# One block of weight sums moved a step forward, and one row load moved from the x products to the y products

## The chip, the cores and the metric

The kernel runs on one core of a Trainium2 chip. The metric is the device time of one execution in microseconds. The kernel before takes 1419.04 us (median of three runs, 1418.62 to 1419.61). The engines that matter here are TensorE (PE, the matrix products), VectorE (DVE), ScalarE (ACT) and SyncE (SP), which issues all transfers. Each engine works through its own list of instructions in order; an instruction that waits holds up all that stand behind it in that list.

## The reference

Two layers are applied one after the other to x, of 2048 rows by 512 columns, each with two sublayers:

```
x = x + A(layernorm(x))     A: y = Cr @ (x @ Dr^T) - Ci @ (x @ Di^T)
x = x + B(layernorm(x))     B: h = gelu(layernorm(x) @ w1); shift four column groups of h
                               by +1, -1, +2, -2 rows; x1 = x + shifted @ w2
                               return x1 + gelu(layernorm(x1) @ w3) @ w4
```

Cr and Ci are the 2048 x 2048 cosine and sine matrices, Dr and Di the 512 x 512 ones; w3 is 512 x 1376 and w4 is 1376 x 512. All is float32.

## The kernel before

**Products in three parts.** Every float32 operand is split into a high part (a cast on ACT) and a low part (a subtraction on DVE), and every product is three matmuls: high by high, high by low, low by high (`mm3`, lines 295 to 297). So PE's work is fixed, and ACT and DVE have to split every operand in time.

**Sublayer A.** The output rows are worked in four chunks of 512 columns (c = 0 to 3). A chunk has first the x products, in steps 0 to 15 (`x_phase`: an even step is two groups of six matmuls into the PSUM banks psc and psb, an odd step one group into psa), and then the y products, k = 0 to 7 (`y_phase`: per k two steps of twelve matmuls, into psc and psd and then psb and psa). Between the x steps of chunks 1 to 3 stand the hidden products of the chunk before, into psd. At the end of the x products ACT copies psc, psb and psa out to SBUF (rr11f L518, rr01f L520, rr00f L526); the first y product writes psc again and so waits for the first of these copies.

**The stream.** The DFT matrices come from HBM in pieces of 512 KB into four buffers (raw0 to raw3), six during the end of the x products and the y products. `stage_one` makes from a piece, or a difference of two (L247, on DVE), what goes into one of four ring slots and casts its high part (L241, L244, L248, on ACT); `stage_two` subtracts to get the low part (L258, on DVE). `stream()` runs this as far ahead as there is a free ring slot. A raw buffer's next load is issued on SP once DVE and ACT have read it.

**Order.** The schedule is written by hand: the order of the calls is the order on each engine. Before each step a `hook` is called, which adds other work at that place. In layer 0 the hook of the x products calls `prepare_at(c, i)`: beside the products of chunks 1 to 3, sums and differences of blocks of w3 and w4 are formed for later. A unit has four parts: `sum_load` (two loads of 256 KB, L1629), `sum_make` (one addition of 512 and two of 256 elements per partition on DVE, L492, and a cast of 1024 on ACT, L1646), `sum_low` (a subtraction of 1024 on DVE, L1650) and `sum_keep` (the store). Chunks 1 and 2 have three units each; the third uses the tile tmp (`sum_t`), which is loaded at x step 11, once tmp's former contents have been stored.

**Rows that come back.** In each layer's last chunk pairs of rows of x are read back from HBM into xs tiles: `BACK` gives the x step and the row. xs[2] (rows 4 and 5) is next read by `norm_z((4, 5))` among the hidden products behind the y products.

Of the kernel before, what the change touches and what calls it, by code (L numbers as in the profile page):

```python
# [21 lines left out]
NC = S // CH  # L22
# [14 lines left out]
WARM = 12  # L37
X6, X7 = 2, 4
HAT = (2, 3, 3, 4, 5, 5, 6, 6)
BACK = {8: 0, 11: 2, 13: 4}  # L40
HORDER = ((1, 0), (0, 1), (1, 1), (0, 0))


# [1 line left out]
def spectral_mlp_kernel(ctx: ExitStack, tc: tile.TileContext, x, ws, hs, w1, w2, w34, out):  # L45
# [10 lines left out]
    x1d = dram.tile([S, D], F32, name="x1d")  # L56
# [28 lines left out]
    def at(name, word, *shape, dtype=F32R):  # L85
        return nc.alloc_sbuf_tensor_at(name, [P, *shape], dtype, offset=base + 4 * word).ap()
# [11 lines left out]
    xs = [at(f"xs{i}", XS + i * 2 * D, 2, D, dtype=F32) for i in range(NP)]  # L98
# [26 lines left out]
    def xt(j):  # L125
        return xs[j // 2][:, j % 2]
# [77 lines left out]
    def rows(sb, d, j, n, load):  # L204
        v = d[j * P : (j + n) * P, :].rearrange("(t p) d -> p t d", p=P)
        nc.sync.dma_start(*((sb, v) if load else (v, sb)))
# [146 lines left out]
    def normed_act(o, s, mr):  # L353
        nc.scalar.activation(o, s, AF.Identity, bias=mr[2], scale=mr[1])
# [100 lines left out]
    late = {}  # L455

    def plain_phase(hook):

        for k in range(NP):
            first, last = k == 0, k == NP - 1  # L460
            a = {"11": ay[k][:, 2], "22": ay[k][:, 3], "21": mid[k % 4][:, 0], "12": mid[k % 4][:, 1]}
            s = stream()
            hook(2 * k)
            jobs = ((PB, a["21"], s[:, 1]), (PA, a["11"], s[:, 1]), (PC, a["12"], s[:, 0]), (PD, a["22"], s[:, 0]))
            if first:
                mm_first(jobs[:2])
                mm_first(jobs[2:])
            else:
                for job in jobs:
                    mm_half(*job, False, False)  # L470
            s = stream()
            hook(2 * k + 1)
            mm_half(PC, a["11"], s[:, 1], False, last)
            mm_half(PD, a["21"], s[:, 1], False, last)
            mm_half(PB, a["22"], s[:, 0], False, last)
            mm_half(PA, a["12"], s[:, 0], False, last)
# [153 lines left out]
    def turn_one(t, q, u):  # L630
        v = t.rearrange("p d (a q j) -> p d a q j", a=NB, q=TC)[:, :, :, q]
        nc.vector.transpose(v, blocks_of(u))

    def turn_out(t, to=None):

        if to is None:
            count["turn"] += 1
            to = zd[count["turn"] % 2]
        z = to.rearrange("(e i) t -> i e t", i=B)
        for b in range(NB):  # L640
            v = t[b * B : (b + 1) * B].rearrange("i d (a t) -> i (d a) t", a=NB)
            nc.sync.dma_start(z[:, :, b * P : (b + 1) * P], v)

    def turn_in(dst):

        z = zd[count["turn"] % 2].rearrange("(d p) t -> p d t", p=P)
        nc.sync.dma_start(dst[:, :, 1], z)
# [971 lines left out]
    sum_t = tmp[:, 0:4].rearrange("p u (a w) -> p u a w", a=2)  # L1619
    sum_t = [(sum_t.bitcast(F32R), sum_t, slice(0, 4))]  # L1620

    def sum_load(kind, k, places):


        src = w34[2 * k : 2 * k + 2, :, 0] if kind == 3 else w34[2 * k + LAG : 2 * k + LAG + 2, :, 1]
        for _, f, v in places:
            for i in range(2):
                if v.start <= 2 * i < v.stop:
                    nc.sync.dma_start(f[:, 2 * i - v.start : 2 * i - v.start + 2, 0], src[i].rearrange("p (a w) -> p a w", a=2))  # L1629

    def sum_make(kind, places):


        raw = [f[:, j, 0] for _, f, v in places for j in range(v.stop - v.start)]
        form = [f[:, j, 1] for _, f, v in places for j in range(v.stop - v.start)]
        r11, r12, r21, r22 = raw if kind == 3 else [raw[i] for i in (0, 2, 1, 3)]
        if len(places) == 1:
            f = places[0][1]
            add(f[:, 0:4:3, 1], r21.unsqueeze(1).broadcast_to([P, 2, 2 * P]), f[:, 0:4:3, 0])
        else:  # L1640
            add(form[0], r21, r11)
            add(form[3], r21, r22)
        add(form[1], form[3], r11)
        add(form[2], form[1], r12)
        for t, f, _ in places:
            nc.scalar.copy(t[:, :, 0], f[:, :, 1])  # L1646

    def sum_low(places):
        for t, f, _ in places:
            nc.vector.tensor_tensor(t[:, :, 1], f[:, :, 1], t[:, :, 0].bitcast(F32), op=ALU.subtract)  # L1650

    def sum_keep(kind, k, places):
        for t, _, v in places:
            if kind == 4:
                nc.sync.dma_start(w4s[k][:, v], t.bitcast(F32))
                continue
            for r in range(2):
                nc.sync.dma_start(w3d[k][:, r, v], t[:, :, r].bitcast(F32))
# [3 lines left out]
    def sum_at(c, kind, k, places, *at_):  # L1662
        todo = (
            lambda: sum_load(kind, k, places),
            lambda: sum_make(kind, places),
            lambda: sum_low(places),
            lambda: sum_keep(kind, k, places),
        )
        for step, f in zip(at_, todo):
            prepare.setdefault((c, step), []).append(f)  # L1670

    def prepare_at(*at_):
        for f in prepare.pop(at_, ()):
            f()

    for c, units in ((1, ((3, 0), (3, 1), (3, 2))), (2, ((3, 3), (3, 4), (4, 0))), (3, ((4, 1), (4, 2)))):
        sum_at(c, *units[0], sum_b, 5 if c == 1 else 0, 8 if c == 1 else 7, 9 if c == 1 else 8, 9)
        sum_at(c, *units[1], sum_a, 1, 10, 11, 12 if c == 3 else 21)
        if c < 3:
            sum_at(c, *units[2], sum_t, 11, 13, 14, 18)  # L1680
    sum_at("hid", 4, 3, sum_b, 0)
    sum_at("hid", 4, 4, sum_r, 2)

    for layer in range(LAYERS):
# [4 lines left out]
        for c in range(NC):  # L1689
            if layer == 0 and c == 0:  # L1690
# [58 lines left out]
                def hook(i):  # L1749
                    k, odd = divmod(i, 2)  # L1750
                    prepare_at(c, i)
                    if not i:
                        second_low(1)
                        xp_stats(1)
                        second_low(0)
                        state["two"] += 1
                        issue_dma()
                        state["limit"] = 4
                        prefetch()
                    state["limit"] = w_items[layer]  # L1760
                    if not odd:
                        if k + 1 < NP:
                            xp_norm(k + 1, 3)
                            xp_main(k + 1)
                        if not k:
                            xp_main_lows(1)
                    else:
                        if 0 < k < NP - 1:
                            xp_main_lows(k + 1)
                        if k + 2 < NP:  # L1770
                            xp_stats(k + 2)
                        if k:
                            xp_sums(k - 1)
                            xp_highs(k - 1, False)
                            xp_lows(k - 1, False)
                    w_split(i)
# [3 lines left out]
            def hook(i):  # L1780
# [34 lines left out]
                if i == 9:  # L1815
                    rows(X0, x1d, j, 2, False)
                if c == NC - 1 and i in BACK:
                    rows(xs[BACK[i] // 2], x1d, BACK[i], 2, True)
                if c == NC - 1 and i == 12:
# [5 lines left out]
            def hook(k):  # L1825
                if layer == 0:
                    prepare_at(c, 2 * NP + k)
                if layer and c == 0:
                    for step, f in zip((1, 1, 2), (ay_sums, ay_highs, ay_lows)):
                        if k == step:  # L1830
                            f(7)
                if k == 1 and c:
                    rows(X1, x1d, (c - 1) * TC + 2, 2, False)
                if c == NC - 1 and k < 2:
                    for q in (2 * k, 2 * k + 1):
                        turn_one(turned0, q, tmp[:, q])
                    for j in (2, 3)[: 2 - 2 * k]:
                        normed_act(tmp[:, j], xt(j), ln2[j])
                if c == NC - 1 and k == 2:
                    turn_out(turned0)  # L1840
                if c == NC - 1 and k == NP - 1:
                    turn_in(ztf[0])

# [86 lines left out]
```

## Time and profile before

| | |
|---|---|
| median of three runs | 1419.04 us |
| the profiled execution's own time | 1418.97 us |
| its span, first to last instruction | 1417.2 us |
| PE busy | 1409.0 us, 99% of the span |
| PE's granted clock | full in all 40 slices |
| DVE busy | 1191.3 us, 84% |
| ACT busy | 765.5 us, 54% |
| transfers | 316.18 MB, mean 223 GB/s |

The span lies 1.8 us under the execution's own time; nothing in the change touches what lies around it. PE is busy nearly throughout, so the time of a stage is PE's work plus the few places where PE stands still. In a timeline a row is: start in us, length in us, engine, line, operation, output and inputs with their shapes, how many instructions are merged, and in brackets the idle time before it with what ended it. Instructions of one engine overlap by a little: the distance of two starts is what an instruction costs its queue. Chunk 1 of layer 0 has its change from x to y products at about 149 us, chunk 2 at 248 us, chunk 3 at 347 us.

### The profile page before, as it was taken

Reading aid. Unit: us, or ns where it says so; the run is one execution under the profiler, and the core shown is the slowest. Engines: PE = TensorE matmul, PEld = TensorE weight load, DVE = VectorE, ACT = ScalarE, POOL = GpSimd, SP = SyncE. Lnnn points to the kernel's source line nnn. Section 1 sums busy time; section 2 is a strip of 40 time slices with the busy share of each in tenths; the row PEclk is TensorE's granted clock in tenths of the full one; section 3 lists DMA queues with packets and bytes.
Section 4 is the critical chain, followed back from the end, with each engine's and each line's share of the span. In section 5 each row is a group of like instructions: output and inputs, shape, how many; then the busy total and the mean of one; then the engine's idle time right before and its main releaser. Section 6 shows DMA issues by size and latency. Waiting matters only on the chain.

```text
span 1417.2 us, 18479 instructions
## 1 busy us (share of the span) xinstructions
PE 1409.0 (99%) x6669; PEld 1181.8 (83%) x6669; DVE 1191.3 (84%) x1684; ACT 765.5 (54%) x1072; POOL 68.2 (5%) x105
## 2 busy tenths in 40 slices
PE   9999999999999999999999999999999999999998
PEld 8888788888788888988888888888888888899887
DVE  7988998998988789956789979879889788897776
ACT  6664555556566655534555545645555566454351
POOL 2100000000001100000000000000000020000000
PEclk9999999999999999999999999999999999999999
DMA  8978858778774748865556476565587457687864
GB/s 290 306 236 302 268 194 274 241 230 309 255 228 146 253 165 264 257 247 180 195 177 218 136 225 206 166 220 170 193 265 237 134 141 245 188 250 252 297 205 160
DMA packets 158907, 316.18 MB, mean 223 GB/s; under 512 B 10848, under 2 KB 78816, under 8 KB 156896
## 3 DMA queue, kind: packets, MB, share of 16 engines
q1 hardware_dynamic: 158816, 315.01, 67.9%
q8 instruction: 52, 0.85, 0.2%
q14 instruction: 39, 0.32, 0.1%
HBM read 260.70 MB, written 54.26 MB: 222 GB/s over the span
## 4 chain that ended last, share of the span: by engine, by line
PE 94%; DVE 3%; DMA 1%; ACT 1%; issue 1%; SPq 0%; POOL 0%; DVEq 0%; ACTq 0%; POOLq 0%
PE psd L295 10%; PE psd L296 10%; PE psd L297 10%; PE psa L295 8%; PE psa L297 8%; PE psa L296 8%; PE psb L296 7%; PE psb L297 7%; PE psb L295 7%; PE psc L295 6%; PE psc L296 6%; PE psc L297 6%; DMA raw<-in_ws 1%; DVE ring L258 1%; DVE rest L492 0%
## 5 line engine op out<-in xcount | busy, mean ns | idle before, releaser
L241 ACT CAST ring<-raw 128x1024 fp32r<-128x1024 f32 x127 | 132.9, 1052 | 69.4 <-PE psd L297 30.6
L258 DVE TENSOR_TENSOR ring<-raw,ring 128x1024 fp32r<-128x1024 f32 x126 | 153.4, 1220 | 14.3 <-ACT ring L241 14.3
L295 PE MATMUL psd<-ring,rr 128*128 128x512 f32 x208 | 80.9, 389 | 0.0
L296 PE MATMUL psd<-ring,rr 128*128 128x512 f32 x208 | 80.9, 389 | 0.0
L297 PE MATMUL psd<-ring,rr 128*128 128x512 f32 x208 | 80.9, 389 | 0.0
L248 ACT CAST ring<-ring0f 128x1024 fp32r<-128x1024 f32 x28 | 29.5, 1054 | 46.9 <-DVE ring0f L247 46.9
L258 DVE TENSOR_TENSOR ring<-ring1f,ring 128x512 fp32r<-128x512 f32 (+1 forms) x56 | 53.3, 952 | 0.8 <-ACT ring L244 0.7
L346 POOL TENSOR_TENSOR rows<-ve,mhalf 128x4 f32<-128x4 f32 x16 | 18.2, 1136 | 735.2 <-DVE ve L345 735.2
L295 PE MATMUL psc<-ring,ay 128*128 128x512 f32 x128 | 50.0, 391 | 1.6 <-ACT rr11f L518 1.6
L296 PE MATMUL psb<-ring,ay 128*128 128x512 f32 x128 | 50.0, 391 | 1.2 <-DVE ring L258 1.2
L297 PE MATMUL psb<-ring,ay 128*128 128x512 f32 x128 | 49.8, 389 | 0.0
L295 PE MATMUL psb<-ring,ay 128*128 128x512 f32 x128 | 49.8, 389 | 0.0
L296 PE MATMUL psc<-ring,ay 128*128 128x512 f32 x128 | 49.8, 389 | 0.0
L297 PE MATMUL psc<-ring,ay 128*128 128x512 f32 x128 | 49.8, 389 | 0.0
L297 PE MATMUL psa<-ring,ay 128*128 128x512 f32 x126 | 49.0, 389 | 0.0
L295 PE MATMUL psa<-ring,ay 128*128 128x512 f32 x126 | 49.0, 389 | 0.0
L295 PE MATMUL psd<-ring,ay 128*128 128x512 f32 x126 | 49.0, 389 | 0.0
L296 PE MATMUL psd<-ring,ay 128*128 128x512 f32 x126 | 49.0, 389 | 0.0
L296 PE MATMUL psa<-ring,ay 128*128 128x512 f32 x126 | 49.0, 389 | 0.0
L297 PE MATMUL psd<-ring,ay 128*128 128x512 f32 x126 | 49.0, 389 | 0.0
L314 POOL TENSOR_TENSOR rs<-ve,mhalf 128x2 f32<-128x2 f32 (+2 forms) x33 | 28.5, 863 | 412.4 <-DVE nb L313 393.4
L697 DVE TENSOR_TENSOR rg<-gt,rg 128x512 fp32r<-128x512 f32 x32 | 22.1, 690 | 29.6 <-ACT rg L696 29.6
(834 smaller groups left out, 4617.1 us busy)
## 6 DMA issues: line engine op xcount, KB each, us to landing
raw<-in_ws SPq DMA_DIRECT2D x183, 512.0 KB, 5.4
raw<-in_hs SPq DMA_DIRECT2D x56, 512.0 KB, 3.7
w3b<-w3d SPq DMA_DIRECT2D x11, 1792.0 KB, 8.5
w4r<-w4d SPq DMA_DIRECT2D x22, 512.0 KB, 3.5
un<-w4s SPq DMA_DIRECT2D x40, 256.0 KB, 3.7
un<-w4d SPq DMA_DIRECT2D x38, 256.0 KB, 4.4
x1d<-tmp SPq DMA_DIRECT2D x12, 512.0 KB, 6.8
xs<-x1d SPq DMA_DIRECT2D x12, 512.0 KB, 5.2
```

The source lines that it names most:

```text
L241: nc.scalar.copy(dest[:, a:b, 0], r[0][:, a:b])
L248: nc.scalar.copy(dest[:, :, 0], lo)
L258: nc.vector.tensor_tensor(lo, src, hi.bitcast(F32), op=ALU.subtract)
L295: nc.tensor.matmul(o, lh, rh, start=first, stop=False, skip_group_check=more)
L296: nc.tensor.matmul(o, lh, rl, start=False, stop=False, skip_group_check=more)
L297: nc.tensor.matmul(o, ll, rh, start=False, stop=last, skip_group_check=more)
L314: nc.gpsimd.tensor_tensor(rs[:, :n], ve[:, :n], mhalf[:, 0, :n], op=ALU.pow)
L346: nc.gpsimd.tensor_tensor(rs, ve, mhalf[:, :, :2], op=ALU.pow)
L697: nc.vector.tensor_tensor(lo, src, hi.bitcast(F32), op=ALU.subtract)
```

## The change

`BACK` loses its entry for x step 13, and rows 4 and 5 are loaded in the hook of the y products at k = 5 (both layers). The third unit's `sum_make` stands at x step 12 instead of 13 and its `sum_low` at 13 instead of 14; its load (11) and its store (18) stay.

```
-BACK = {8: 0, 11: 2, 13: 4}
+BACK = {8: 0, 11: 2}
...
         if c < 3:
-            sum_at(c, *units[2], sum_t, 11, 13, 14, 18)
+            sum_at(c, *units[2], sum_t, 11, 12, 13, 18)
...
                 if c == NC - 1 and k == 2:
                     turn_out(turned0)
+                if c == NC - 1 and k == 5:
+                    rows(xs[2], x1d, 4, 2, True)
```

On DVE at the end of chunk 1's x products the order changes so (the same rows change in chunk 2). The ring slots are ring_172, 174, 176 and 178, their float views ring0f, 1f, 2f and 3f; tmp is the third unit's tile; ring0f and ring1f are made for the first two y steps.

```order
 L258 TENSOR_TENSOR ring_176<-raw_183,ring_176 128x2x512
+L492 TENSOR_TENSOR tmp<-tmp 128x2x256
+L492 TENSOR_TENSOR tmp<-tmp 128x256 x2
 L247 TENSOR_TENSOR ring0f<-raw_181,raw_180 128x2x512
 L258 TENSOR_TENSOR ring_178<-ring3f,ring_178 128x512
-L492 TENSOR_TENSOR tmp<-tmp 128x2x256
-L492 TENSOR_TENSOR tmp<-tmp 128x256 x2
+L1650 TENSOR_TENSOR tmp<-tmp 128x4x256
 L247 TENSOR_TENSOR ring1f<-raw_181,raw_180 128x2x512
 L258 TENSOR_TENSOR ring_172<-ring0f,ring_172 128x2x512
-L1650 TENSOR_TENSOR tmp<-tmp 128x4x256
```

The additions move from in front of ring1f to in front of ring0f, and the subtraction L1650 from behind ring1f to in front of it. On ACT the cast of tmp (L1646) moves by one place, from in front of ring1f's cast to in front of ring0f's.

On SP in the last chunk of layer 0, before, around the load of rows 4 and 5 into xs_147 (raw_184 and raw_185 are the two further buffers):

```order
L1655 DMA w4s_87<-suma 128x2048
L1598 DMA w3d_83<-tmp 256x1x256
L206 DMA xs_147<-x1d 128x2x512
L223 DMA raw_184<-in_ws 128x1024
L223 DMA raw_185<-in_ws 128x1024
L223 DMA raw_180<-in_ws 128x1024
```

and of the change, at the place where that load now stands:

```order
L642 DMA zd_73<-turned_153 32x16x128 x4
L223 DMA raw_182<-in_ws 128x1024
L223 DMA raw_183<-in_ws 128x1024
L206 DMA xs_147<-x1d 128x2x512
L223 DMA raw_180<-in_hs 128x1024
L223 DMA raw_181<-in_hs 128x1024
```

The load has passed behind twelve loads of the stream, a store of rows and the four stores of turned_153; raw_184 now follows directly on w3d_83. In layer 1 it passes likewise, to behind the second of the four loads from in_hs.

## Rows read from the trace of the kernel before

**Rows 1.** PE's waits, longest first: in total, times, longest (us).

```profile
PE psc L295 <- ACT rr11f L518: 1.6, 2, 0.8
PE psb L296 <- DVE ring L258: 1.2, 1, 1.2
```

**Rows 2.** Timeline of PE, start of chunk 1's y products.

```profile
149.31 0.50 PE L295 MATMUL psc<-ring,ay 128*128 128x512 f32 x1 [0.76 <-ACT rr11f L518]
```

**Rows 3.** Timeline of ACT at the same place.

```profile
147.72 1.05 ACT L248 CAST ring<-ring1f 128x1024 fp32r<-128x1024 f32 x1
148.68 1.07 ACT L518 COPY rr11f<-psc 128x512 f32<-128x512 f32 x2
```

**Rows 4.** Timeline of DVE at the same place.

```profile
141.65 1.22 DVE L258 TENSOR_TENSOR ring<-raw,ring 128x1024 fp32r<-128x1024 f32 x1
143.15 1.23 DVE L247 TENSOR_TENSOR ring0f<-raw,raw 128x1024 f32<-128x1024 f32 x1 [0.28 <-PE psb L297]
144.29 0.68 DVE L258 TENSOR_TENSOR ring<-ring3f,ring 128x512 fp32r<-128x512 f32 x1
144.90 1.60 DVE L492 TENSOR_TENSOR tmp<-tmp 128x512 f32<-128x512 f32 x3
146.42 1.22 DVE L247 TENSOR_TENSOR ring1f<-raw,raw 128x1024 f32<-128x1024 f32 x1
...
148.69 1.22 DVE L1650 TENSOR_TENSOR tmp<-tmp 128x1024 fp32r<-128x1024 f32 x1
```

**Rows 5.** Chunk 1: transfers issued at 135.2 us (KB each, us to landing).

```profile
tmp<-in_w SPq DMA_DIRECT2D x2, 256.0 KB, 7.2
```

**Rows 6.** Timeline of PE, start of chunk 2's y products.

```profile
248.42 0.50 PE L295 MATMUL psc<-ring,ay 128*128 128x512 f32 x1 [0.82 <-ACT rr11f L518]
```

**Rows 7.** Timeline of DVE, end of chunk 2's x products.

```profile
240.80 1.23 DVE L258 TENSOR_TENSOR ring<-raw,ring 128x1024 fp32r<-128x1024 f32 x1
...
245.53 1.22 DVE L247 TENSOR_TENSOR ring1f<-raw,raw 128x1024 f32<-128x1024 f32 x1
```

**Rows 8.** Chunk 2: transfers issued at 236.8 us.

```profile
tmp<-in_w SPq DMA_DIRECT2D x1, 256.0 KB, 6.6
```

**Rows 9.** Timeline of PE, chunk 3's y products, layer 0.

```profile
354.50 0.39 PE L297 MATMUL psd<-ring,ay 128*128 128x512 f32 x1
354.73 0.39 PE L295 MATMUL psb<-ring,ay 128*128 128x512 f32 x1
356.27 0.50 PE L296 MATMUL psb<-ring,ay 128*128 128x512 f32 x1 [1.15 <-DVE ring L258]
...
361.62 0.39 PE L295 MATMUL psb<-ring,ay 128*128 128x512 f32 x1
362.07 0.50 PE L296 MATMUL psb<-ring,ay 128*128 128x512 f32 x1
```

**Rows 10.** Timeline of DVE at the same place.

```profile
350.99 1.30 DVE L632 STREAM_TRANSPOSE turned<-tmp 128x512 f32<-128x512 f32 x2
353.86 1.23 DVE L247 TENSOR_TENSOR ring0f<-raw,raw 128x1024 f32<-128x1024 f32 x1 [1.57 <-DMA raw<-in_ws]
355.00 1.22 DVE L258 TENSOR_TENSOR ring<-ring3f,ring 128x1024 fp32r<-128x1024 f32 x1
```

**Rows 11.** Chunk 3: transfers issued at 345.6 us, and at 346.6 us.

```profile
raw<-in_ws SPq DMA_DIRECT2D x1, 512.0 KB, 6.9
...
raw<-in_ws SPq DMA_DIRECT2D x1, 512.0 KB, 7.1
```

**Rows 12.** Stretches: us, busy of PE, PEld, DVE, ACT, POOL; clock; DMA share; GB/s.

```profile
344.00:353.80 9.80, 9.80 (x45) 8.12 (x44) 7.61 (x8) 7.50 (x11) 0.00 (x0) 1.00 0.97 343
376.50:380.20 3.70, 3.70 (x18) 3.05 (x17) 3.70 (x5) 1.34 (x2) 0.00 (x0) 1.00 0.01 2
1077.90:1078.90 1.00, 1.00 (x6) 0.82 (x5) 1.00 (x2) 0.00 (x0) 0.00 (x0) 1.00 0.00 0
```

**Rows 13.** All transfers of line 1629.

```profile
DMA to landing us min/median/max: 3.7/5.3/7.4
```

## The prediction, made before the change was run

> **What bounds the kernel now.** I read the page first: PE is busy for 99% of the span at full clock, so the time can only move where PE stands still. PE's waits come next. Apart from the one at the start there are two on ScalarE's copy of psc (rr11f, 1.6 us together) and one on a low part in the ring (1.2 us) [rows 1]. The timelines place them. The two are at the ends of the x products of chunks 1 and 2, where the change moves the sums [rows 2, 6]; the third is in the y products of layer 0's chunk 3, behind the row load that the change moves [rows 9]. So each part of the change aims at a hold that exists, and what has to be found is whether the holds shrink or grow.
>
> What the holds cost now: matmuls start 0.23 us apart (354.50, 354.73). In chunk 3 the next starts at 356.27, so 1.54 - 0.23 = 1.31 us are lost, which the row shows as 1.15 of idle time because a matmul's 0.39 overlaps the next by 0.16; and the first matmul behind a hold lasts 0.50, which adds 0.11: 1.42 us. A second, small hold costs 362.07 - 361.62 - 0.23 + 0.11 = 0.33 [rows 9]. Reckoned alike, the hold of chunk 1 costs 0.76 + 0.16 + 0.11 = 1.03 and that of chunk 2 1.09 [rows 2, 6]. All four together are 3.9 us; that is the most that these places can give.
>
> **Part 1, the sums.** No work is added or removed; three additions, one cast and one subtraction stand earlier on their queues. The question is what the copy of psc waits for. On ScalarE it stands right behind the cast of ring1f, which ends when it may start (147.72, then 148.68) [rows 3]. That cast starts when DVE has made ring1f (146.42 + 1.22 = 147.64) [rows 3, 4]. The chain is therefore: ring1f on DVE, its cast, the copy, PE at 149.31. PE comes 149.31 - 146.42 = 2.89 us behind the start of ring1f, and I carry this distance over.
>
> Now the start of ring1f, counted on DVE from the low part of ring_176 at 141.65. An operation of 1024 elements keeps the queue for 1.14 us (143.15 to 144.29), the low part of 512 for 0.61 (144.29 to 144.90), the three additions for 1.52 (144.90 to 146.42) [rows 4]. L1650 has the length of the other 1024-element operations, 1.22 us, so it too costs 1.14 [rows 4]. Before, behind 142.79 there stood an idle 0.28 or a little more for a ring slot, then ring0f, the low part of ring3f and the additions: 146.42. Now there stand additions, ring0f, low part and, new in this stretch, L1650: 142.79 + 1.52 + 1.14 + 0.61 + 1.14 = 147.20. The idle time is filled, but the subtraction that used to come behind ring1f has come in front of it. ring1f starts 0.78 us later, and so does the copy, and so does PE: **+0.8 us in chunk 1**. The additions need their load there: issued at 135.2, landing 7.2 us later, at about 142.4, before DVE comes to it at 142.79 [rows 5]. It is a margin of only 0.3 us.
>
> In chunk 2 this margin is gone. DVE is done with its low part at 240.80 + 1.14 = 241.94 [rows 7], but the load was issued at 236.8 and takes 6.6 us: 243.4 [rows 8]. Before, the additions stood behind two operations and found it landed. Now DVE stands until about 243.5, and ring0f, the low part of ring3f and ring1f stand behind the waiting addition. ring1f starts at 243.5 + 1.52 + 1.14 + 0.61 + 1.14 = 247.9 instead of 245.53 [rows 7]: **+2.4 us in chunk 2**. The low part of ring3f, which the last x step needs, comes late too, but PE's loss there lies ahead of the same copy and is inside the 2.4, not beside it.
>
> Behind these places nothing is added: in the y products DVE has the subtraction behind it already, the loads that wait for ring1f are late by no more than PE is, and the sums' store stays at step 18. The bounds of part 1: if the load comes as in the other chunk (6.6 or 7.2 us), chunk 1 stays at +0.8, since DVE is then the later one, and chunk 2 goes to +3.0; half a microsecond earlier there gives +1.9. So +2.7 to +3.8, with +3.2 taken.
>
> At this place a rule of the Trainium skill speaks for the change. DMA: Bandwidth & Descriptors, section "Anatomy of one DMA — SWDGE (gpsimd) path", puts a transfer (issued from GpSimd; these are SP's) at about 2.0 us fixed plus its bytes at 436 GB/s: as an estimate 2.6 us for 256 KB. By that the load would be there long before DVE in both chunks, and chunk 2 would cost what chunk 1 costs: a sum of +0.2 instead of +1.8. The trace differs, with 6.6 and 7.2 us at these two places [rows 5, 8].
>
> **Part 2, the row load.** Layer 0's chunk 3 is short of transfers: from 344.0 to 353.8 the DMA share is 0.97 at 343 GB/s [rows 12], and DVE waits 1.57 us for a piece of the matrix before it can make ring0f at 353.86 [rows 10]. That piece is the load issued at 346.6 with 7.1 us to landing, 353.7 [rows 11]. The row load of 512 KB stands in front of it. At 343 GB/s it takes 524288 B / 343000 B per us = 1.5 us of this full stretch; the two pieces issued at 345.6 and 346.6, as large, landed at 352.5 and 353.7, 1.2 us apart [rows 11]. With it gone ring0f can start 1.2 to 1.5 us earlier, and not before the two transposes are done at 352.3 [rows 10], which is 1.6 earlier at most. The hold at 356.27 ends with the low part of ring3f, 355.00 + 1.22 = 356.22, and PE would need it at 354.96 [rows 9, 10]: 1.26 us earlier and the hold is gone. The second hold at 362.07 hangs on the same row of DVE operations, so PE cannot come out of it by more than DVE has moved. From 1.2 to 1.6, then; I take **-1.4 us**, between the two prices of 512 KB.
>
> What the load costs at its new place: it comes behind the last piece of the y products. In layer 0 the DMA share from 376.5 to 380.2 is 0.01, and 512 KB fits there; in layer 1 the share just before the next two loads is 0.00 [rows 12]. Its reader is a product group later. I cost it at nothing in both layers; without that cover it would push the next loads by 1.2 to 1.5 us, and PE by no more than that. In layer 1 no PE wait exists to be won [rows 1].
>
> **Sum.** +0.8 + 2.4 - 1.4 = +1.8 us on the profiled execution's own 1418.97: 1420.77. The median lies 0.07 above that execution, so 1420.8. Behind these places PE is busy, so the shift reaches the end. With the bounds (+2.7 to +3.8, less 1.2 to 1.6) the forecast's own range is 1420.1 to 1421.6. A measurement of this kernel tells about 0.2% from no change, 2.8 us: below 1416.2 is faster, above 1421.9 slower. The forecast is a small loss inside that.
>
> **Rivals.**
> The sums get out of the way (faster): the additions fill DVE's idle time before ring0f [rows 4] and ScalarE's cast of tmp leaves the place right before ring1f's cast, so both holds on the copy vanish, -1.03 - 1.09, and part 2 brings 1.4: 1415.5. It needs ring1f to start some 0.9 us earlier than at 146.42. Against it stands the order: L1650 is in front of ring1f now, and no idle time of 0.28 us pays for 1.14. 8%.
>
> The load is early (no change): transfers of this line landed in 3.7 to 7.4 us, 5.3 in the middle [rows 13]. At 5.1 or less in chunk 2 it is there when DVE comes, and that chunk costs +0.8 only: 0.8 + 0.8 - 1.4 = +0.2, 1419.2. The page DMA: Bandwidth & Descriptors of the Trainium skill would have it so. Against: the queue in front of the load is the same as before. 9%.
>
> Part 2 brings nothing (slower): the piece for ring0f is held by something other than the row load, as the transfer of w4s or its own issue on SP, and DVE still waits until 353.7. Then part 1 stands alone: +3.2, 1422.2. It decides from the point where part 2 gives under 0.4 us. For it: the store and the loads ahead of it in this stretch are not taken away, and the piece before it was issued only at 345.6. Against: the DMA engines are full there [rows 12], so that 512 KB less must show. 11%.
>
> **Chances.** Forecast 72% (61 of it within 0.2%; 11 slower, where the sums' load lands later than the 7.2 us of chunk 1 or part 2 gives little), early load 9, faster 8, part 2 nothing 11 (2 of it still within). Faster 0.08, within 0.2% 0.72, slower 0.20. The range takes in the early load and part 2 without effect, with some room for a later load: 1418.3 to 1422.7.
>
> **What the profile after would show.** In chunk 1: DVE's additions at 142.8 without a wait, ring1f at about 147.2, PE's wait on rr11f 1.5 us instead of 0.76. In chunk 2: DVE waits about 1.5 us for the load of tmp, PE is short of ring3f's low part for about 0.7 us and then waits on rr11f again; from the last free x step to the first y step 2.4 us more than now. In chunk 3: the 1.57 us before ring0f fall to 0.3 or less and PE's 1.15 us to under 0.2. The forecast is wrong if PE's waits on rr11f are shorter than before, or if chunk 3's wait stays.

## The result, and the profile after

The kernel before takes 1419.14 us (median of 8 runs, 1418.62 to 1419.61), the changed one 1422.48 us (8 runs, 1421.00 to 1425.38): a ratio of 1.0025, 95% interval 1.0014 to 1.0036. It is slower by 3.3 us, and its runs spread over 4.4 us where those of the kernel before spread over 1.0. The profiled execution is its fastest, 1421.0 us with a span of 1419.2. A second set of eleven runs (below) gives +2.7 instead of +3.3, so the size of the loss is known to about half a microsecond.

PE's waits of the changed kernel, against [rows 1]:

```profile
PE psc L295 <- ACT rr11f L518: 3.7, 2, 2.2
PE psb L296 <- DVE ring L258: 0.5, 1, 0.5
```

The two waits on the copy of psc have grown from 1.6 to 3.7 us together, and the one on the ring's low part has shrunk from 1.2 to 0.5. Both parts of the change can be seen, the first as a loss and the second as a gain.

DVE at the end of chunk 1's x products, against [rows 4], and PE, against [rows 2]:

```profile
141.81 1.22 DVE L258 TENSOR_TENSOR ring<-raw,ring 128x1024 fp32r<-128x1024 f32 x1
142.95 1.60 DVE L492 TENSOR_TENSOR tmp<-tmp 128x512 f32<-128x512 f32 x3
144.47 1.22 DVE L247 TENSOR_TENSOR ring0f<-raw,raw 128x1024 f32<-128x1024 f32 x1
145.61 0.68 DVE L258 TENSOR_TENSOR ring<-ring3f,ring 128x512 fp32r<-128x512 f32 x1
146.21 1.21 DVE L1650 TENSOR_TENSOR tmp<-tmp 128x1024 fp32r<-128x1024 f32 x1
147.34 1.22 DVE L247 TENSOR_TENSOR ring1f<-raw,raw 128x1024 f32<-128x1024 f32 x1
```

```profile
150.23 0.50 PE L295 MATMUL psc<-ring,ay 128*128 128x512 f32 x1 [1.52 <-ACT rr11f L518]
```

From the low part at 141.81 DVE runs without a gap, and ring1f starts 5.53 us behind it; before it was 146.42 - 141.65 = 4.77. PE follows 2.89 us behind ring1f, as before, and its idle time goes from 0.76 to 1.52.

The same in chunk 2, against [rows 7] and [rows 6]:

```profile
241.56 1.22 DVE L258 TENSOR_TENSOR ring<-raw,ring 128x1024 fp32r<-128x1024 f32 x1
243.39 1.61 DVE L492 TENSOR_TENSOR tmp<-tmp 128x512 f32<-128x512 f32 x3 [0.60 <-DMA tmp<-in_w]
...
247.79 1.22 DVE L247 TENSOR_TENSOR ring1f<-raw,raw 128x1024 f32<-128x1024 f32 x1
```

```profile
250.68 0.50 PE L295 MATMUL psc<-ring,ay 128*128 128x512 f32 x1 [2.22 <-ACT rr11f L518]
```

DVE now waits for the sums' load. It was issued at 237.2 and took 6.0 us; the first row answers to [rows 8]. The second is SP's own wait in front of that load, for the landing of a store of what tmp held before:

```profile
tmp<-in_w SPq DMA_DIRECT2D x1, 256.0 KB, 6.0
...
SPq L1629 <- DMA x1d<-tmp: 2.5, 1, 2.5
```

In chunk 3, against [rows 9] and [rows 10], the wait of PE is shorter but not gone, because the piece for ring0f still comes late (issued at 347.7, landing 355.2; the bracket of ring0f names PE, which had long been done):

```profile
357.74 0.50 PE L296 MATMUL psb<-ring,ay 128*128 128x512 f32 x1 [0.45 <-DVE ring L258]
...
363.08 0.39 PE L295 MATMUL psb<-ring,ay 128*128 128x512 f32 x1
363.53 0.50 PE L296 MATMUL psb<-ring,ay 128*128 128x512 f32 x1
```

```profile
355.32 1.23 DVE L247 TENSOR_TENSOR ring0f<-raw,raw 128x1024 f32<-128x1024 f32 x1 [1.36 <-PE psa L297]
```

In this one execution the three places make +0.76, +1.4 (2.22 against 0.82 idle) and -0.7; its time is 2.0 us over that of the profiled execution before. That is 0.6 more than the sum; it lies behind PE's last matmul, in the last stores to out. The median is another 1.5 us higher, which this profile does not explain.

### The profile page after: what moved, and what is told of

The parts are those of the page before. It is cut to its first block, busy times and chain, and to the rows that moved or that the text cites. A ratio compares the mean times of both kernels' runs of the same rounds, so it can differ in the third digit from the quotient of the medians.

```text
span 1419.2 us, 18483 instructions
## 1 busy us (share of the span) xinstructions
PE 1409.0 (99%) x6669; PEld 1181.8 (83%) x6669; DVE 1191.2 (84%) x1684; ACT 764.9 (54%) x1072; POOL 67.3 (5%) x105
## 4 chain that ended last, share of the span: by engine, by line
PE 95%; DVE 3%; DMA 1%; ACT 1%; issue 1%; SPq 0%; POOL 0%; DVEq 0%; ACTq 0%; POOLq 0%
PE psd L295 10%; PE psd L296 10%; PE psd L297 10%; PE psa L297 8%; PE psa L295 8%; PE psa L296 8%; PE psb L296 7%; PE psb L297 7%; PE psb L295 7%; PE psc L295 6%; PE psc L296 6%; PE psc L297 6%; DVE ring L258 0%; DMA x1d<-tmp 0%; DMA tmp<-in_w 0%
## 5 line engine op out<-in xcount | busy, mean ns | idle before, releaser
L248 ACT CAST ring<-ring1f 128x1024 fp32r<-128x1024 f32 x28 | 29.5, 1054 | 35.4 <-DVE ring1f L247 35.4
```

The source lines that it names most:

```text
L248: nc.scalar.copy(dest[:, :, 0], lo)
```

## Experiments

The theory: L1650 in front of ring1f costs 0.8 us in chunk 1; in chunk 2 the sums' load holds DVE, so PE's start follows its landing; the row load in chunk 3 gives something back; and the spread comes from chunk 2. Its rivals: the row load at its new place is what costs; it is the additions and not L1650; the spread comes from the clock or from something else. The medians below are over 11 runs where nothing else is said; the kernel before had 1418.81 to 1418.89 beside them.

**Each part alone.** The sums without the row load's move, against the kernel before:

```diff
 BACK = {8: 0, 11: 2, 13: 4}
...
-            sum_at(c, *units[2], sum_t, 11, 13, 14, 18)
+            sum_at(c, *units[2], sum_t, 11, 12, 13, 18)
```

Expected: 

> Only the sums are moved; the row load of the last chunks stays at x step 13. Theory (the sums cost): VectorE's subtraction L1650 in front of ring1f costs 0.8 us in chunk 1, and in chunk 2 VectorE stands for the sums' load, whose landing moves from run to run, so that the time is +2.3 us or more over the kernel before, 1421.4 to 1425, with a spread between runs of 2 us or more; PE's waits on rr11f are 1.5 and over 2 us, and PE resumes about 7.4 us after that load has landed. Rival (the row load costs): the runs of the change that lie over 1421 come from the row load at its new place; then this kernel is at most +2.3, with the small spread of the kernel before (1 us).

Measured: 1423.09 us (8 runs, 1420.53 to 1424.56), ratio 1.0026, interval 1.0016 to 1.0036. The sums are the loss and the spread. In its profile (1423.95 us) PE waits 2.15 us in chunk 2, and the granted clock is at half some time behind that wait (columns as in [rows 12], the clock is the third number from the end):

```profile
251.45 0.50 PE L295 MATMUL psc<-ring,ay 128*128 128x512 f32 x1 [2.15 <-ACT rr11f L518]
...
253.00:256.00 3.00, 3.00 (x9) 2.33 (x8) 2.45 (x3) 2.72 (x4) 0.00 (x0) 0.52 0.64 184
```

The loss of 4.2 us in the median is 0.5 more than the two longer holds of this profile (2.1) and one such fall of the clock (1.6, see below) make; that stays open.

The row load's move without the sums, against the kernel before:

```diff
-BACK = {8: 0, 11: 2, 13: 4}
+BACK = {8: 0, 11: 2}
...
             sum_at(c, *units[2], sum_t, 11, 13, 14, 18)
...
+                if c == NC - 1 and k == 5:
+                    rows(xs[2], x1d, 4, 2, True)
```

Expected: 

> Only the row load of the last chunks is moved; the sums stay at steps 13 and 14. Theory (the sums cost): -0.7 to -1.4 us, 1417.7 to 1418.4, with a spread of about 1 us; the wait on the low part of ring3f in chunk 3 falls from 1.15 us to 0.5 or less, and the waits on rr11f stay at 0.8. Rival (the row load costs): about 1419 to 1421 with a spread of 2 us or more, and a new wait late in a layer's last chunk.

Measured: 1418.42 us (1417.26 to 1419.10), ratio 0.9996, interval 0.9987 to 1.0005: -0.5 us, less than the 0.7 to 1.4 expected, and the interval does not tell it from nothing. In its profile (1417.26 us, its fastest run) the list of PE's waits has none in chunk 3 left; beside the one at the start it holds only

```profile
PE psc L295 <- ACT rr11f L518: 1.5, 2, 0.8
```

The rival that the load costs at its new place is ruled out.

**The change a second time.** No edit.

Expected: 

> The change as it is, a second time, for its spread and for a second profile. Theory: median 1421 to 1424, spread 2 us or more; in chunk 2 the load of tmp lands at another time than in the first profile, and PE's first y product comes 7.4 us behind the landing again. Rival (something else moves the time): the landing and the wait in chunk 2 are as in the first profile while the time differs.

Measured: 1421.55 us (1420.22 to 1425.29), ratio 1.0022, interval 1.0013 to 1.0031; eight runs from 1420.2 to 1422.0 and three from 1424.3 to 1425.3. In the profile (1420.22 us) the load was issued at 236.2 and took 5.9 us:

```profile
tmp<-in_w SPq DMA_DIRECT2D x1, 256.0 KB, 5.9
```

It landed at 242.1 and the additions start at 242.20; PE's wait is 1.66 us, between chunk 1's and that of the first profile.

**L1650 put back.** The additions stay at step 12. This edit and those after it are against the change, but for the doubled row load.

```diff
-            sum_at(c, *units[2], sum_t, 11, 12, 13, 18)
+            sum_at(c, *units[2], sum_t, 11, 12, 14, 18)
```

Expected: 

> The change, but the subtraction L1650 stays at step 14, behind ring1f, and only the additions are at step 12. Theory: 1.14 us less stand in front of ring1f, so PE's step into the y products is 0.7 to 0.8 us in chunk 1 (1.15 before, 1.9 in the change) and 0.9 to 1.5 in chunk 2, by the landing of the sums' load; 1418.0 with a spread of 1.5 to 2 us. Rival (it is the additions and their wait alone that cost): chunk 1 stays at 1.9 and the time at 1421 or more.

Measured: 1418.44 us (1417.11 to 1422.16; the highest of the eleven stands 2 us above the next, and what it met is not known; even without it the runs spread over 3.0 us, more than expected). DVE and PE in chunk 1:

```profile
142.62 1.61 DVE L492 TENSOR_TENSOR tmp<-tmp 128x512 f32<-128x512 f32 x3
144.14 1.22 DVE L247 TENSOR_TENSOR ring0f<-raw,raw 128x1024 f32<-128x1024 f32 x1
145.27 0.69 DVE L258 TENSOR_TENSOR ring<-ring3f,ring 128x512 fp32r<-128x512 f32 x1
145.88 1.22 DVE L247 TENSOR_TENSOR ring1f<-raw,raw 128x1024 f32<-128x1024 f32 x1
```

```profile
148.77 0.50 PE L295 MATMUL psc<-ring,ay 128*128 128x512 f32 x1 [0.39 <-ACT rr11f L518]
```

With L1650 behind ring1f the wait is 0.39 us, half of that before; with it in front it was 1.52. The difference, 1.13, is one operation of 1024 elements. So it is L1650, and the additions by themselves are a small gain where their load has landed (0.76 to 0.39 us in chunk 1).

**Chunk 1 only.** In chunk 2 the sums stand as before.

```diff
-            sum_at(c, *units[2], sum_t, 11, 12, 13, 18)
+            sum_at(c, *units[2], sum_t, 11, *((12, 13) if c == 1 else (13, 14)), 18)
```

Expected: 

> The change, but the sums at steps 12 and 13 in chunk 1 only; in chunk 2 they are at 13 and 14 as before. Theory (chunk 1 costs 0.8 us by the place of L1650, the spread comes from chunk 2's load and the clock that falls behind a hold of over 2 us): the row load alone gave 1418.4, so 1419.2 here, with a spread of about 1.5 us; PE's step into the y products is 1.9 us in chunk 1 and 1.1 to 1.2 in chunk 2, and the clock stays at full. Rival (a hold of 1.9 us is enough to let the clock fall, or chunk 1 makes the spread): 1420.5 or more, with runs 2 us above others.

Measured: 1419.20 us (1418.61 to 1420.29). That is 0.8 over the row load alone, with 1.52 us of wait in chunk 1 and 0.75 in chunk 2, and the spread is gone (1.7 us, against 1.5 of the kernel before).

**The load made early.** In chunk 2 four stores are taken out of the queue ahead of it.

```diff
-        sum_at(c, *units[0], sum_b, ..., 9 if c == 1 else 8, 9)
+        sum_at(c, *units[0], sum_b, ..., 9 if c == 1 else 8, 12 if c == 2 else 9)
```

Expected: 

> The change, but in chunk 2 the first unit's four stores of 256 KB, which stand ahead of the sums' load in the queue, are issued at x step 12 instead of 9, behind that load. Theory (in chunk 2 it is the landing of the load that holds VectorE): the load is issued and lands 2 us or more earlier, VectorE does not wait, and the step into chunk 2's y products is 1.9 us as in chunk 1; 1419.5 to 1421 with a spread of 1.5 us, and no half clock. Rival (the load is not what holds it, or the stores only change places with it): step of 2 us or more and the time of the change, 1421.5 to 1423.

Measured: 1419.27 us (1418.50 to 1420.33), ratio 0.9999, interval 0.9990 to 1.0008; 0.2 below the range expected. Transfers issued at 234.3 us, then DVE and PE in chunk 2:

```profile
tmp<-in_w SPq DMA_DIRECT2D x1, 256.0 KB, 5.7
```

```profile
241.29 1.22 DVE L258 TENSOR_TENSOR ring<-raw,ring 128x1024 fp32r<-128x1024 f32 x1
242.43 1.61 DVE L492 TENSOR_TENSOR tmp<-tmp 128x512 f32<-128x512 f32 x3
```

```profile
249.72 0.50 PE L295 MATMUL psc<-ring,ay 128*128 128x512 f32 x1 [1.52 <-ACT rr11f L518]
```

The load lands at 240.0, two microseconds before DVE comes, DVE does not wait, and chunk 2 has the 1.52 us that chunk 1 has in the profiles of the change. Nothing but the place of four stores in the queue was changed, and the time fell by over 2 us: it is the landing that held chunk 2. In this one profile chunk 1 shows the same thing the other way: there its load landed at 142.6, later than in the profiles of the change, DVE stood 0.22 us for it, and PE waited longer:

```profile
149.98 0.50 PE L295 MATMUL psc<-ring,ay 128*128 128x512 f32 x1 [1.83 <-ACT rr11f L518]
```

The margin of 0.3 us that the prediction saw in chunk 1 is thus not always there.

**A longer hold in chunk 2.** The three additions are made twice there, with the same values.

```diff
+        for _ in range(2 if places is sum_t and k == 0 else 1):
             ...                    (the additions of sum_make)
```

Expected: 

> The change, with the three additions of chunk 2's third unit done twice over (the second time gives the same values). Theory (behind a hold of over 2 us the clock falls in some runs, and 1.5 us of matmuls are lost by it): the step into chunk 2's y products grows by 1.5 to 3.5 to 4.2 us, and the clock falls in most runs behind it: 1423.5 to 1426, with the granted clock at about half for some us after that hold in the profile. Rival (the slow runs of the change come from something else): 1421.5 + 1.5 = 1423 in the middle, with the same two groups of runs as in the change.

Measured: 1423.49 us (5 runs, 1421.13 to 1424.85), at the lower edge of what was expected and not far from the rival's 1423, so that the time alone does not decide. The profile does. The stretches of its profile before, behind and after the hold, columns as in [rows 12] (the clock is the third number from the end):

```profile
248.00:251.30 3.30, 0.94 (x4) 0.40 (x3) 3.30 (x4) 1.51 (x3) 0.00 (x0) 1.00 0.16 45
251.30:254.80 3.50, 3.42 (x8) 2.78 (x9) 3.50 (x4) 3.50 (x8) 0.00 (x0) 0.51 0.73 263
254.80:258.00 3.20, 3.20 (x15) 2.63 (x15) 2.58 (x3) 1.53 (x2) 0.00 (x0) 1.00 0.80 228
```

PE stood still for most of the first stretch: the longest wait in it is 2.44 us, as part of the added time had been spent in a wait of 0.79 us before it. In the second its clock is at 0.51, that is 1.2 GHz instead of 2.4, and only 8 matmuls run in 3.5 us where 15 do in the 3.2 us after it.

**The change three times more, one profile each.**

Expected of the first: 

> The change once more, for one more profile with its own time. Theory (the runs over 1423 us are those in which the clock falls behind chunk 2's hold): a time over 1423 goes with a stretch of half clock behind that hold, a time under 1422 with none; VectorE's additions start 0.1 us and PE's y products 7.4 us behind the landing of the sums' load. Rival (the spread comes from elsewhere): a time over 1423 with full clock throughout, or the reverse.

Expected of the others: 

> As for the run before: over 1423 us with a stretch of half clock behind chunk 2's hold, under 1422 without; rival: no such tie.

 And: 

> As for the two runs before: over 1423 us with a stretch of half clock behind chunk 2's hold, under 1422 without; rival: no such tie.

Measured: 1422.55, 1420.29 and 1422.49 us. The first, at 1422.55, stretches from PE's last x product on:

```profile
247.70:250.70 3.00, 0.59 (x3) 0.14 (x1) 3.00 (x4) 1.55 (x3) 0.00 (x0) 1.00 0.24 81
250.70:251.40 0.70, 0.67 (x3) 0.59 (x4) 0.70 (x2) 0.70 (x2) 0.00 (x0) 0.95 0.92 322
251.40:254.70 3.30, 3.30 (x10) 2.52 (x9) 3.30 (x3) 3.30 (x6) 0.00 (x0) 0.50 0.59 207
254.70:258.00 3.30, 3.30 (x16) 2.73 (x15) 2.39 (x3) 1.36 (x2) 0.00 (x0) 0.99 0.89 293
```

and its matmuls when the clock is at half:

```profile
250.73 0.50 PE L295 MATMUL psc<-ring,ay 128*128 128x512 f32 x1 [2.44 <-ACT rr11f L518]
...
251.68 0.63 PE L295 MATMUL psc<-ring,ay 128*128 128x512 f32 x1
252.10 0.63 PE L296 MATMUL psc<-ring,ay 128*128 128x512 f32 x1
252.53 0.63 PE L297 MATMUL psc<-ring,ay 128*128 128x512 f32 x1
```

The second, at 1420.29, in the corresponding stretch:

```profile
250.40:253.70 3.30, 3.30 (x16) 2.73 (x15) 3.30 (x4) 3.30 (x6) 0.00 (x0) 1.00 0.71 225
```

Matmuls start 0.43 us apart instead of 0.23 for some eight of them: 8 x 0.2 = 1.6 us lost, beyond the hold. The third (1422.49) has the same fall behind a wait of 2.34 us:

```profile
250.10:253.50 3.40, 3.35 (x8) 2.68 (x9) 3.40 (x4) 3.40 (x7) 0.00 (x0) 0.50 0.77 281
```

So of the five profiles of the change the two at 1422.5 have it and the three at 1420.2 to 1421.0 don't. The bound of 1423 us in the expectation was set too high, as both fell just under it; the tie itself holds. In the four profiles of the change in which DVE waits for the load, PE's first y product comes 7.42 us behind its landing each time (here 243.31 and 250.73), and in the second of the three profiles here, where it landed before DVE came, the wait is chunk 1's 1.52.

**The row load doubled.** The kernel before, with a second row load of 512 KB behind the first in chunk 3.

```diff
                     rows(xs[BACK[i] // 2], x1d, BACK[i], 2, True)
+                    if i == 13 and layer == 0:
+                        rows(xs[3], x1d, 6, 2, True)
```

Expected: 

> The kernel before, with a second row load of 512 KB (rows 6 and 7, which are loaded again later as before) behind the one at x step 13 of layer 0's last chunk. Theory (the matrix pieces stand in line behind it, 1.2 to 1.5 us for 512 KB): the hold on ring3f's low part in chunk 3 grows from 1.15 to 2.4 to 2.7 us, and the time to 1420.1 to 1420.5. Rival (transfers there are bound otherwise): within 0.5 us of before.

Measured: 1420.95 us (1419.28 to 1423.56), ratio 1.0017, interval 1.0008 to 1.0026. PE in chunk 3:

```profile
357.57 0.50 PE L296 MATMUL psb<-ring,ay 128*128 128x512 f32 x1 [2.35 <-DVE ring L258]
```

and the stretches behind it:

```profile
357.50:358.70 1.20, 1.13 (x5) 0.96 (x6) 1.20 (x3) 0.01 (x1) 0.00 (x0) 1.00 0.99 406
358.70:362.10 3.40, 3.40 (x10) 2.63 (x9) 3.40 (x6) 2.03 (x4) 0.00 (x0) 0.51 0.77 196
```

512 KB more made the hold 1.2 us longer, as the spacing of two pieces of that size had said (1.2 us) [rows 11]. The time grew by 2.1, 0.5 more than the top of what was expected, and here too the clock falls to half behind a hold of over 2 us, in another chunk and without the sums' move.

**The sums in the y products.** The version that the experiments point to: additions and subtraction behind the copies.

```diff
-            sum_at(c, *units[2], sum_t, 11, 12, 13, 18)
+            sum_at(c, *units[2], sum_t, 11, 16, 17, 18)
```

Expected: 

> The change, but with the third unit's additions at step 16 and its subtraction at step 17, that is in the first two y products, behind ring1f and behind the copies of psc and psb. Theory: neither the additions, nor the cast, nor L1650 stand in front of ring1f's cast and the copy, so both waits on rr11f are gone, -1.0 and -1.1, and with the row load's -0.7 to -1.4 the time is 1415.6 to 1416.4, with a spread of 1 us. Rival (VectorE has no room in the y products): 2.7 us of additions and subtraction there make a later low part late, and 1 us or more comes back as waits on a low part in the ring: 1417 or more.

Measured: 1416.39 us (1415.83 to 1417.30), ratio 0.9981, interval 0.9972 to 0.9990: 2.5 us faster than the kernel before and 5 to 6 faster than the change. ACT and PE at the end of chunk 1's x products:

```profile
145.74 1.05 ACT L248 CAST ring<-ring1f 128x1024 fp32r<-128x1024 f32 x1 [0.68 <-DVE ring1f L247]
146.70 1.06 ACT L518 COPY rr11f<-psc 128x512 f32<-128x512 f32 x2
```

```profile
147.70 0.39 PE L297 MATMUL psa<-ring,ax 128*128 128x512 f32 x1
147.93 0.39 PE L295 MATMUL psc<-ring,ay 128*128 128x512 f32 x1
```

The copy is done before PE wants psc, and PE goes from x to y without a wait, in both chunks. DVE had the room in the y products; only chunk 3's wait is left (0.5 us).

## Why the prediction was right or wrong

The time, 1422.48, lies inside the range that was given (1418.3 to 1422.7), near its top, and the sign of the shift was right. The size was not: +1.8 was forecast, in a range of its own from 1420.1 to 1421.6, and +3.3 measured, which lies just past 0.2%, on the side that was given 0.20 and not on the one that was given 0.72. That the time still lies inside the wide range is in part luck. That range was made for an early load and for a part 2 without effect; what filled it was a term that the forecast did not have, the clock, while the loss in chunk 2 and the gain of part 2 were both smaller than forecast. As an estimate from what follows: 0.8 + 1.4 - 0.5 = +1.7 in an execution with a full clock, and 1.6 more, +3.3, in one with the fall. The first eight runs have their median at the latter, the eleven later ones (+2.7) between the two.

*Chunk 1, +0.8*: right. Idle time went from 0.76 to 1.52 us, ring1f came where the sum of starts put it (147.34, with the low part 0.16 later than before, against 147.20), and putting L1650 back took it away.

*Chunk 2, +2.4*: the mechanism was right, the size too large; +1.4 in the profile of the change. The step that failed is the one that added the two losses, as if the load moved with PE. PE and DVE came to chunk 2 later by chunk 1's loss, but the load waits on SP for the landing of a store and landed at 243.2, as before at 243.4. ring1f started at 247.79, where the prediction had it (247.9); but of the distance from 245.53 chunk 1 had already paid its 0.8. DVE waited 0.60 us for the load and not 1.5. One landing would prove little, as it scatters by over a microsecond, but other profiles say the same: counted from the end of PE's last x product in chunk 1, the load landed 94.1 to 94.9 us later in the three profiles that wait about 0.75 us there, and 93.8 to 95.2 in the eight that wait 1.52. In the profile with L1650 put back, which waits 0.39, it is 93.0, so that it moves along a little is not excluded. In the profiles of the change the landing lies between 242.1 and 243.3, and PE's wait between 1.52 and 2.44 us. By the figures of the Trainium skill ("DMA: Bandwidth & Descriptors", section "Anatomy of one DMA — SWDGE (gpsimd) path", which is about transfers issued from GpSimd) such a transfer is estimated at 2.6 us, which would have made it early; these traces don't agree, with 5.9 and 6.0 us. With the queue ahead of the load shortened, chunk 2's loss fell to chunk 1's, as the early rival had it.

*Part 2, -1.4*: the price of 512 KB was right (1.2 us more when doubled). The step from it to the gain failed, that without the row load ring0f starts 1.2 to 1.5 us earlier. Counted from the issue of the store of w3d that stands in front of it on SP, ring0f starts after 10.34 us in the kernel before and 10.59 with the sums alone. Without the row load it starts after 8.75 and 8.87 us in two profiles (the row load alone and L1650 put back), and after 9.42 to 10.07 in the other nine, 0.3 to 0.9 us earlier than before. In the first profile of the change the piece for ring0f was issued 1.1 us earlier by this count (1.98 against 3.11 us) but took 7.6 us to land instead of 7.1. DVE's wait for it, forecast to fall from 1.57 to 0.3 or less, was 1.36, and PE's 0.45 instead of under 0.2: the sign of being wrong that the prediction gave, that chunk 3's wait stays, came true by half. In the median part 2 gives 0.5 us, which is not clear of noise, and the profiles with the load moved show chunk 3's wait at nothing to 0.9 us. What else holds the piece, and why only in some executions, stays open. That the load costs nothing at its new place was right: no profile shows a wait of PE there.

*The term that was missing*: the clock. The forecast took a hold to cost its own length and 0.11 us for the first matmul. Behind holds of 2.15 us and more the granted clock fell to half in most executions that were profiled, and about 1.6 us more are lost. The profiles of the change with a full clock there stand at 1420.2 to 1421.0 us and those with the fall at 1422.5, which fits with the first profile, with a full clock, lying under the median. Of the runs of the change above 1424 us no profile was taken. In the second set the three of them have a mean granted clock of 0.997, against 0.998 to 1.000 in the other eight runs, which speaks for the clock; but a run at 1424.56 us with the sums alone has 0.999. So that the clock makes these runs too is argued and not shown.

Of the rivals the first, that the sums get out of the way, fell with its own condition: ring1f came later, not earlier. That the load is early held in one profile of the change (landed at 242.3, DVE there at 242.5, late by chunk 1's loss) and where the queue in front of it was shortened. That part 2 brings nothing comes nearest to the measured time, 1422.2. Its reason, that something other than the row load holds the piece for ring0f, is borne out in part; but the +3.2 us of the sums that it adds were not there as holds (0.8 and 1.4), and the clock made up for it.

## What to carry to other kernels

Before side work is moved on an engine's list, ask of each operation whether it crosses the one that the critical copy waits for, and which way. Here the additions stood in front of it before and after, and gained 0.4 us by filling idle time; one subtraction passed from behind to in front of it and cost 1.13 us; and the cure was to move all of it behind the copy. An operation that is moved ahead of its operand's landing puts the scatter of a transfer's landing on the path, and everything behind it on that queue pays. When two waits lie in a row, reckon the second against absolute landing times, since a transfer that waits for other transfers need not move along with the engines. And the price of a transfer taken away in a full stretch is not yet the gain: the next one was issued 1.1 us earlier and landed only in part so.

## What the runs showed of the hardware that was not expected

A hold of PE of 2.15 to 2.44 us was followed by a granted clock of one half (1.2 GHz) in five profiles (two of the change, the sums alone, the longer hold, the doubled row load), each time beginning about at PE's restart or up to 1.2 us behind it, and for some eight matmuls; in one profile of the change a wait of 2.22 us was not followed by it, and waits of 1.83 us or less never were, in the fourteen profiles here. It costs 1.6 us beside the hold itself. What decides between the two outcomes at the same length stays open. And a transfer of 256 KB in the same place of the same program landed 5.7 to 6.6 us behind its issue from one execution to another, which is enough to move this kernel's time by a microsecond once an engine waits for it.
